# Loads of the first 256 tokens on a hardware queue, and an output product in thirds: a retention layer with a bilinear feed-forward on one core

## The chip, the core and the metric

The kernel runs on one core of a Trainium2 chip. The core has a matrix engine (PE, with its weight loads shown apart as PEld), a vector engine (DVE), a scalar engine (ACT), a general engine (POOL) and a queue engine (SP), and 16 DMA engines. Loads that POOL issues go through the software queue [...]; loads that SP issues go through the hardware queue [...]. The metric is the time on the device in microseconds; before the change it is 335.84, the median of four runs (335.33 to 339.21).

## The reference

```
scores = q @ k^T / 8                  # 8 batches, 8 heads, 576 positions, 64 per head
ret    = (scores * Dmat) @ v          # Dmat[i, j] = gamma_h ** (i - j) for i >= j, else 0
x      = ret, heads side by side      # 4608 tokens x 512
out    = ((x @ w_a) * (x @ w_b)) @ w_out     # 512 -> 1536 -> 512
```

gamma of head h is 1 - 2^(-5-h). Inputs and output are fp32. The kernel multiplies in bf16 and sums in fp32. It splits the decay: v is scaled by gamma^-j, q (or the result) by gamma^i/8, and a mask of zeros and ones keeps i >= j. So a running sum of k^T v (the *state*) carries everything from earlier positions of the batch.

## The kernel before

The 4608 tokens are 36 chunks of 128. Chunks 0 to 3 are the *fresh* ones, handled as two *units* of 256 tokens, two neighbouring tokens to a partition (e = 0, 1). The later chunks go in pairs through `kv` (state sums), `stage1` (scores, and what comes from the state), `stage2` (scores times v, then the scaling into xT). The feed-forward takes 9 blocks of 512 tokens: `ffn_ab` makes, for each of 12 slices F of the 1536 inner columns, `pa` and `pb` (4 matmuls each), copies pa on ACT and multiplies on DVE into hT; `ffn_out` then makes four products `po` of 128 tokens, 12 matmuls each against w_out.

Everything is scheduled by hand: each engine executes its instructions in the order of the program, and an instruction waits until what it reads is there and what it overwrites is free.

The start is one straight sequence (lines 161 to 171 issue the first loads, lines 606 to 652 the rest). For unit 0: 9 idle products, transposes of q, an idle product, transposes of k, two idle products, scores, state; then unit 1 the same way, with the first three F of block 0 between, in halves of 256 tokens. Before the change q of unit 0 is loaded as bf16 (line 141, POOL) and is scaled as it leaves PSUM, with `qs0`, a table of 128 x 4 x 256 made by four exps on ACT (line 206):

```
    nc.vector.tensor_tensor(q_out, tq.rearrange("p c e t -> p c t e"),
                            qs0.rearrange("p c (t e) -> p c t e", e=2),
                            op=ALU.mult)
```

POOL's queue holds, in this order: q and k of unit 0, three index tables (`ramp`, line 151), the second half of v of unit 0, a table, q, k and v of unit 1, the weights of F 0 and of F 1, 2 (line 118, four loads each), the scaling of v of unit 1 (line 479), the remaining weights in three groups, w_out in one load of 3 MB (line 124), then chunks 4 to 9, v, q, k each. The first half of v of unit 0 is SP's only load.

From F 3 of block 0 on, a list `todo` with due costs sets what goes between the matmuls. A matmul of 512 columns counts 1; when the count passes an entry's cost, at an edge (after an F in `ffn_ab`, after every fourth matmul in `ffn_out`), the entry is put into the program. Block 0's `ffn_ab` ends at 96, its `ffn_out` at 144. `pop` puts single steps of the state sums at further places. Chunks 4 and 5 enter inside the first `ffn_out`: the scaling of v on DVE and `transposes` (16 on PE, copied out by ACT and DVE, lines 277 and 278) at 110 and 112, the state product at 116, `first` and `second` (stage1, stage2) at 128 and 136.

PSUM has 8 buffers of one bank: 4 in `ps_ffn` (pa, pb, po, and before the change the transposes `tp`), 2 in `ps_x` (state products and scores), 2 in `ps_o`.

Of the kernel before, what the change touches and what calls it, by code (L numbers as in the profile page):

```python
# [18 lines left out]
def kernel(  # L19
# [117 lines left out]
    def load_fresh_qk(u):  # L137
        t = [nat.tile([128, 2, DM], BF16, tag="qk", name="fqk")
             for _ in (0, 1)]
        for w, src in ((0, q), (1, k)):  # L140
            nc.gpsimd.dma_start(  # L141
                t[w].rearrange("p a b -> p (a b)").rearrange(
                    "p (h x) -> p h x", h=H),
                src[0, :, 256 * u:256 * u + 256, :].rearrange(
                    "h (p e) d -> p h (e d)", e=2))
        fresh[u] = [x.rearrange("p a b -> p (a b)").rearrange(
            "p (h e d) -> p h e d", h=H, e=2) for x in t]
# [13 lines left out]
    load_fresh_v(0, 0, 4, nc.sync)  # L161
    load_fresh_qk(0)
# [3 lines left out]
    load_fresh_v(0, 4, 8, nc.gpsimd)  # L166
    ramp(posf[:, 4 + MID + 1:NPOS], [[128, PER - MID - 1]], 64, 1)
    load_fresh_qk(1)
# [14 lines left out]
    lgq = const.tile([128, HP], FP32)  # L183
    for p in range(HP):
        for r in (0, 1):
            nc.vector.memset(lgq[64 * r:64 * r + 64, p:p + 1],
                             math.log(gammas[2 * p + r]))
# [16 lines left out]
    qs0 = const.tile([128, HP, 256], FP32)  # L204
    for p in range(HP):
        nc.scalar.activation(qs0[:, p], idx[:, 0:256], AF.Exp,
                             bias=biasq[:, 0:1], scale=lgq[:, p:p + 1])
# [6 lines left out]
    def make_keep2():  # L214
        for e in (0, 1):
            nc.vector.tensor_copy(rowf[:, e:e + 1], posf[:, 2 * e:2 * e + 1])
            nc.vector.tensor_scalar_add(
                rowf[64:128, e:e + 1], rowf[64:128, e:e + 1], -128.0)
            nc.vector.tensor_scalar(keep2[:, e, :], idx[:, 0:128],
                                    rowf[:, e:e + 1], None, op0=ALU.is_ge)  # L220
# [42 lines left out]
    def transposes(i, by_dma):  # L263
        qk = qk_of[i]
        qkT = qkt_pool.tile([128, 2, HP, 128], BF16, tag="qkT", name="qkT")
        qkt_of[i] = qkT
        if by_dma:
            nc.sync.dma_start_transpose(
                qkT.rearrange("p w c t -> p (w c) t"),
                qk.rearrange("p w e -> p (w e)"))  # L270
            return
        tp = ps_ffn.tile([128, 2, HP, 128], BF16, tag="ab", name="tp")
        for w in (0, 1):
            for p in range(HP):
                nc.tensor.transpose(tp[:, w, p, :],
                                    qk[:, w, p * 128:(p + 1) * 128], identity)
        nc.scalar.copy(qkT[:, 0], tp[:, 0])
        nc.vector.tensor_copy(qkT[:, 1], tp[:, 1])
# [152 lines left out]

    def ffn_out(blk):
        hT = hT_of.pop(blk)
        for u in range(4):
# [25 lines left out]
            osb = o_pool.tile([128, DM], FP32, tag="osb", name="osb")  # L460
            if u % 2 == 0:
                nc.scalar.copy(osb, po)  # L462
            else:
                nc.vector.tensor_copy(osb, po)  # L464
            nc.sync.dma_start(out[tok:tok + 128, :], osb)
# [8 lines left out]
    def fresh_vscale(u, h0, h1, eng):  # L474
# [3 lines left out]
        for e in (0, 1):  # L478
            eng.tensor_tensor(  # L479
                fv[u][e].rearrange("p (h d) -> p h d", h=H)[:, h0:h1, :],  # L480
                vf2[:, u, :].rearrange("p (h e d) -> p h e d", h=H, e=2)[
                    :, h0:h1, e, :],
                vs_all[:, 2 * e + u, h0:h1].unsqueeze(2).to_broadcast(
                    [128, h1 - h0, D]), op=ALU.mult)

    def fresh_transposed(u, w, p0, p1, place):
        tp = place[0].tile([128, p1 - p0, 2, 128], BF16, tag=place[1],
                           name="ftp")
        for p in range(p0, p1):
            for e in (0, 1):  # L490
                for r in (0, 1):
                    nc.tensor.transpose(
                        tp[half(r), p - p0, e, :],
                        fresh[u][w][:, 2 * p + r, e, :], identity)
# [14 lines left out]
    def fresh_kv(u, s):  # L509
        for p in range(HP):  # L510
            for e in (0, 1):
                for r in (0, 1):
# [3 lines left out]
                        fresh[u][1][half(s), h, e, :],  # L516
# [82 lines left out]
    def settled(u, n=1, w=128):  # L599
        for _ in range(n):  # L600
# [7 lines left out]
    fresh_vscale(0, 0, 4, nc.vector)  # L608
    q_out, k_out = fresh_tiles(0)
    tq = fresh_transposed(0, 0, 0, HP, AB)  # L610
    idle_products(1)
    tk = [fresh_transposed(0, 1, 0, 2, AB), fresh_transposed(0, 1, 2, 4, X)]
    make_keep2()
    nc.vector.tensor_tensor(q_out, tq.rearrange("p c e t -> p c t e"),
                            qs0.rearrange("p c (t e) -> p c t e", e=2),
                            op=ALU.mult)
    nc.scalar.copy(k_out[:, 0:2], tk[0])
    nc.vector.tensor_copy(k_out[:, 2:4], tk[1])
    make_qs(256, 512)
    idle_products(2)  # L620
    fresh_vscale(0, 4, 8, nc.vector)
# [5 lines left out]
    tk = fresh_transposed(1, 1, 0, HP, AB)  # L627
    fresh_state1(0)
    fresh_kv(0, 1)
    nc.scalar.copy(k_out, tk)  # L630
# [6 lines left out]
    fresh_stage2(0)  # L637
    fresh_scores(1, (X, O))
# [14 lines left out]
    load_wo(0, NF)  # L653
# [26 lines left out]
    def second(g):  # L680
        flush()
        stage2(units[g])
        if 4 <= g + 2 < len(units):
            kv(units[g + 2], nc.scalar)

    load(*range(4, 10))
    todo = [(110, vscale, (4, nc.vector)), (110, vscale, (5, nc.vector)),
            (110, transposes, (4, False)), (112, transposes, (5, False)),
            (116, kv, (units[0], nc.scalar)),
            (128, first, (0,)), (136, second, (0,)),  # L690
            (136, vscale, (6, nc.gpsimd)), (136, vscale, (7, nc.gpsimd)),
            (142, transposes, (6, False)), (148, transposes, (7, False)),
            (152, kv, (units[1], nc.scalar)),
# [29 lines left out]
    run(ffn_out(0))  # L723
# [38 lines left out]
```

## Time and profile before

| | |
|---|---|
| time of the profiled execution | 336.14 us |
| its span, first to last instruction | 334.4 us |
| all runs | 336.14, 339.21, 335.54, 335.33 us |
| granted PE clock | 1.00 throughout |
| PE busy | 318.6 us, 95% of the span |
| PE busy from 0 to 10, 10 to 20, 20 to 30 us | 8.10, 8.22, 9.55 us |
| PE busy from 40 to 50, 60 to 70 us | 7.89, 8.41 us |
| first pa of F 3, all 512 tokens | 23.68 us |
| first po | 40.61 us |
| w_out load, issue to landing | 14.9 us |

The time is the span and what lies around it. A line of the waits reads: engine, what it would run, what it waited for: total, times, longest. A line of the timeline reads: start, duration, engine, line, operation, result and operands, shape and count; in brackets how long the engine stood idle before, and what released it. Some matmul records are missing, so a count may be short. A DMA line on POOL is its issue only, not the transfer.

### The profile page before, as it was taken

The numbers are of one execution on the slowest core, as the hardware profiler recorded it, in microseconds if no ns is written. First come the engines' busy times: TensorE is split into PE (matmuls) and PEld (weight loads), VectorE is DVE, ScalarE is ACT, GpSimd is POOL, SyncE is SP. The second block draws the span as 40 slices with busy tenths as digits, with TensorE's granted clock in tenths as the row PEclk, the third lists the DMA queues.
The fourth block names the chain that finished last, engine by engine and source line by source line (L and its number), as shares of the span: only waits on it lengthen the run. The fifth ranks groups of instructions, "written<-read, shape, count | busy, mean of one in ns | idle before, by whom it ended". The sixth has DMA issues, their size and how long they took to land.

```text
span 334.4 us, 8797 instructions
## 1 busy us (share of the span) xinstructions
PE 318.6 (95%) x3705; PEld 166.7 (50%) x3746; DVE 165.4 (49%) x324; ACT 112.7 (34%) x233; POOL 143.9 (43%) x176
## 2 busy tenths in 40 slices
PE   7889889989999999999999999999999999999995
PEld 3564346868544444445444544454444444444443
DVE  6754336757554555356445644454445534444321
ACT  4737524545143213332332223322323133203321
POOL 8786297878658795508350837072100000000000
PEclk9999999999999999999999999999999999999999
DMA  9999999999999999906999499939900700020002
GB/s 144 202 159 191 217 178 233 172 133 159 183 187 181 131 157 239 177 1 89 121 204 96 79 115 217 98 56 136 190 0 28 132 34 1 12 86 31 2 31 94
DMA packets 116151, 40.94 MB, mean 122 GB/s; under 512 B 102992, under 2 KB 109392, under 8 KB 116112
## 3 DMA queue, kind: packets, MB, share of 16 engines
q0 software_dynamic: 80688, 23.34, 68.3%
q1 hardware_dynamic: 35280, 16.95, 27.6%
q8 instruction: 29, 0.48, 0.6%
q10 hardware_dynamic: 144, 0.10, 0.1%
q14 instruction: 10, 0.08, 0.1%
HBM read 37.75 MB, written 9.44 MB: 141 GB/s over the span
## 4 chain that ended last, share of the span: by engine, by line
PE 83%; DMA 10%; POOL 3%; issue 2%; DVE 0%; ACT 0%; POOLq 0%; ACTq 0%
PE po L453 25%; PE pa L414 25%; PE pb L422 25%; DMA wo_sb<-in_moe_w_out_dram 4%; DMA vf<-in_v_dram 2%; DMA wa_sb<-in_moe_w_a_dram 2%; PE o L339 2%; PE o L381 2%; PE kv L294 2%; DMA qk<-in_k_dram 1%; PE sc L359 1%; POOL fqk L141 1%; PE po L442 1%; POOL fvb L479 1%; POOL wb_sb L118 1%
## 5 line engine op out<-in xcount | busy, mean ns | idle before, releaser
L427 DVE TENSOR_TENSOR hT<-ha,pb 128x512 bf16<-128x512 bf16 (+1 forms) x123 | 76.5, 622 | 100.5 <-PE pb L422 86.9
L414 PE MATMUL pa<-xT,wa_sb 128*128 128x512 bf16 (+1 forms) x477 | 113.0, 353 | 3.0 <-issue 1.8
L422 PE MATMUL pb<-xT,wb_sb 128*128 128x512 bf16 (+1 forms) x491 | 113.4, 353 | 0.1
L419 ACT CAST ha<-pa 128x512 bf16<-128x512 f32 (+1 forms) x123 | 65.7, 534 | 124.6 <-PE pa L414 123.4
L453 PE MATMUL po<-wo_sb,hT 128*128 128x512 bf16 x395 | 91.1, 379 | 4.3 <-issue 2.7
L422 PEld LDWEIGHTS <-wb_sb 128*128 128x128 bf16 x492 | 48.1, 98 | 45.3 <-issue 0.3
L414 PEld LDWEIGHTS <-wa_sb 128*128 128x128 bf16 x492 | 46.8, 98 | 47.0 <-issue 3.0
L256 POOL TENSOR_TENSOR vb<-vf,vs_all 128x512 bf16<-128x512 f32 x30 | 31.6, 1060 | 76.7 <-PE o L339 42.0
L453 PEld LDWEIGHTS <-hT 128*128 128x128 bf16 x420 | 39.0, 98 | 45.9 <-DMA wo_sb<-in_moe_w_out_dram 1.7
L462 ACT COPY osb<-po 128x512 f32<-128x512 f32 x18 | 10.6, 586 | 75.1 <-PE po L453 75.1
L102 POOL DMA_DIRECT2D qk<-in_q_dram x36 | 31.1, 867 | 7.0 <-DMA wo_sb<-in_moe_w_out_dram 6.4
L110 POOL DMA_DIRECT2D vf<-in_v_dram x36 | 31.9, 889 | 1.5 <-issue 1.0
L102 POOL DMA_DIRECT2D qk<-in_k_dram x36 | 31.1, 872 | 1.1 <-DMA vf<-in_v_dram 0.5
L367 DVE TENSOR_TENSOR sT<-sc,keep 128x512 bf16<-128x512 f32 x32 | 20.6, 684 | 12.1 <-PE sc L359 12.1
L398 DVE TENSOR_TENSOR xT<-o,qs 128x512 bf16<-128x512 f32 x32 | 20.6, 684 | 11.8 <-PE o L339 10.7
L307 DVE TENSOR_TENSOR s<-kv,s 128x256 f32<-128x256 f32 x49 | 20.5, 419 | 5.8 <-ACT sbf L317 4.5
L317 ACT CAST sbf<-s 128x256 bf16<-128x256 f32 x56 | 21.1, 406 | 3.1 <-DVE s L305 2.7
L464 DVE COPY osb<-po 128x512 f32<-128x512 f32 x17 | 11.7, 687 | 19.3 <-PE po L453 19.3
L339 PE MATMUL o<-qkT,sbf 64*64 64x64 bf16 x456 | 12.1, 195 | 0.1
L339 PEld LDWEIGHTS <-sbf 64*64 64x64 bf16 x456 | 8.2, 108 | 5.7 <-issue 5.5
L381 PEld LDWEIGHTS <-vb 64*64 64x64 bf16 x512 | 6.4, 108 | 6.6 <-issue 6.6
L381 PE MATMUL o<-sT,vb 64*64 64x64 bf16 x512 | 8.1, 195 | 0.0
(75 smaller groups left out, 128.5 us busy)
## 6 DMA issues: line engine op xcount, KB each, us to landing
out_dram<-osb SPq DMA_DIRECT2D x35, 256.0 KB, 4.6
vf<-in_v_dram POOLq DMA_DIRECT2D x29, 256.0 KB, 6.4
qk<-in_q_dram POOLq DMA_DIRECT2D x28, 128.0 KB, 6.5
qk<-in_k_dram POOLq DMA_DIRECT2D x28, 128.0 KB, 7.0
wo_sb<-in_moe_w_out_dram POOLq DMA_DIRECT2D x1, 1536.0 KB, 14.9
wa_sb<-in_moe_w_a_dram POOLq DMA_DIRECT2D x6, 192.0 KB, 6.7
wb_sb<-in_moe_w_b_dram POOLq DMA_DIRECT2D x6, 192.0 KB, 7.7
vf<-in_v_dram POOLq DMA_DIRECT2D x8, 128.0 KB, 7.4
```

The costliest lines, as they stand in the source:

```text
L102: nc.gpsimd.dma_start(t[r0:r0 + n, w, :].rearrange("p (h d) -> p h d", h=H), src[b, :, s0:s0 + n, :].rearrange("h s d -> s h d"))
L110: nc.gpsimd.dma_start(t[r0:r0 + n, :].rearrange("p (h d) -> p h d", h=H), v[b, :, s0:s0 + n, :].rearrange("h s d -> s h d"))
L256: eng.tensor_tensor(vb.rearrange("p (h d) -> p h d", h=H), vf.rearrange("p (h d) -> p h d", h=H), vs[:, i % PER, :].unsqueeze(2).to_broadc ...
L317: nc.scalar.copy(sb, new)
L339: nc.tensor.matmul(o[s][half(c), ci, j, :], st[half(r), p, :], qkt_of[i][half(r), 0, p, half(s)], start=start, stop=True, skip_group_check ...
L367: nc.vector.tensor_tensor(sT[:, r].rearrange("p n c t -> p (n c) t"), sc[r].rearrange("p n c t -> p (n c) t"), keep.unsqueeze(1).to_broadc ...
L381: nc.tensor.matmul(o[s][half(c), ci, j, :], vb[half(s), 64 * h:64 * h + 64], sT[half(s), h % 2, ci, h // 2, :], start=False, stop=True, sk ...
L414: nc.tensor.matmul(pa[:, 0:n], wa_sb[:, c, fs], xT[:, c, tok0:tok0 + n], start=(c == 0), stop=(c == NC - 1))
L419: nc.scalar.copy(ha[:, 0:n], pa[:, 0:n])
L422: nc.tensor.matmul(pb[:, 0:n], wb_sb[:, c, fs], xT[:, c, tok0:tok0 + n], start=(c == 0), stop=(c == NC - 1))
L427: nc.vector.tensor_tensor(hT[:, F, off:off + n], ha[:, 0:n], pb[:, 0:n], op=ALU.mult)
L453: nc.tensor.matmul(po, hT[:, F, u * 128:(u + 1) * 128], wo_sb[:, F, :], start=(F == 0), stop=(F == NF - 1))
```

## The change

1. q of unit 0 is loaded as fp32 by SP (`fq32`), and all of v of unit 0 behind it by SP; POOL loads k first and has neither. q is multiplied by its decay on DVE as it becomes bf16, before its transposes, with the small table `qv` (128 x 2 x 8); the transposes are then copied out unscaled, half by ACT and half by DVE. `qs0` and its constants are gone. The mask's row numbers come from POOL.
2. In the start, v of unit 0 is scaled in two instructions of 128 x 512 for four of 128 x 256, the second unit's k transposes come after the state product, in two buffers, and two of the four `make_qs` exps go to ACT after unit 0's xT.
3. w_out is loaded in thirds of 4 slices F, with chunk 4 (v, q, k) after the first and chunk 5 after the second. The output of block 0 is summed in the same thirds: 4 matmuls for each of four po, then the next third; all four po are open at once and are stored in the last third.
4. Chunks 4 and 5 are transposed in `ps_x`; those of chunk 4 come due at 90, which is after the last F (96), ahead of the output product, those of chunk 5 still at 112. v of chunk 5 and some entries for chunks 6 and 7 move by a few counts.

```diff
+    fq32 = const.tile([128, 2 * DM], FP32)
...
+    def load_fresh_qk(u, w):
+
+        t = nat.tile([128, 2, DM], BF16, tag="qk", name="fqk")
+        flat = t.rearrange("p a b -> p (a b)")
+        if u == 0 and w == 0:
+            nc.sync.dma_start(fq32.rearrange("p (h x) -> p h x", h=H),
+                              fresh_src(w, u))
+        else:
+            nc.gpsimd.dma_start(flat.rearrange("p (h x) -> p h x", h=H),
+                                fresh_src(w, u))
...
-    load_fresh_v(0, 0, 4, nc.sync)
-    load_fresh_qk(0)
+    load_fresh_qk(0, 0)
+    load_fresh_v(0, 0, 8, nc.sync)
+    load_fresh_qk(0, 1)
     ramp(idx[:, 0:512], [[1, 512]], 0, 0)
     ramp(posf[:, 0:4], [[1, 2], [256, 2]], 0, 2)
     ramp(posf[:, 4:4 + MID + 1], [[128, MID + 1]], 0, 1)
-    load_fresh_v(0, 4, 8, nc.gpsimd)
+    for c in (0, 1):
+        ramp(rowf[64 * c:64 * c + 64, 0:2], [[1, 2]], 0, 2)
+    load_fresh_qk(1, 0)
     ramp(posf[:, 4 + MID + 1:NPOS], [[128, PER - MID - 1]], 64, 1)
-    load_fresh_qk(1)
+    load_fresh_qk(1, 1)
     load_fresh_v(1, 0, 8, nc.gpsimd)
...
-    qs0 = const.tile([128, HP, 256], FP32)
-    for p in range(HP):
-        nc.scalar.activation(qs0[:, p], idx[:, 0:256], AF.Exp,
-                             bias=biasq[:, 0:1], scale=lgq[:, p:p + 1])
+    qv = const.tile([128, 2, H], FP32)
+    nc.vector.tensor_tensor(
+        qv, posf[:, 0:4:2].unsqueeze(2).to_broadcast([128, 2, H]),
+        lgv.unsqueeze(1).to_broadcast([128, 2, H]), op=ALU.mult)
+    nc.scalar.activation(qv, qv, AF.Exp, bias=biasq[:, 0:1], scale=-1.0)
...
+    def ffn_out_parts(blk, parts):
+
+        hT = hT_of.pop(blk)
+        po = [ps_ffn.tile([128, 512], FP32, tag="ab", name="po")
+              for _ in range(4)]
+        for f0, f1 in parts:
+            for u in range(4):
+                for F in range(f0, f1):
+                    nc.tensor.matmul(po[u], hT[:, F, u * 128:(u + 1) * 128],
+                                     wo_sb[:, F, :],
+                                     start=(F == 0), stop=(F == NF - 1))
+                    if F < f1 - 1:
+                        yield 1.0, False
+                if f1 == NF:
+                    store(512 * blk + 128 * u, po[u], u)
+                pop()
+                yield 1.0, True
...
-    fresh_vscale(0, 0, 4, nc.vector)
+    make_keep2()
+    for h0 in (0, 4):
+        nc.vector.tensor_tensor(
+            fresh[0, 0][:, h0:h0 + 4],
+            fq32.rearrange("p (h e d) -> p h e d", h=H, e=2)[:, h0:h0 + 4],
+            qv.rearrange("p e h -> p h e")[:, h0:h0 + 4].unsqueeze(3)
+            .to_broadcast([128, 4, 2, D]), op=ALU.mult)
     q_out, k_out = fresh_tiles(0)
-    tq = fresh_transposed(0, 0, 0, HP, AB)
+    tq = [fresh_transposed(0, 0, 0, 2, AB), fresh_transposed(0, 0, 2, 4, X)]
     idle_products(1)
+    nc.scalar.copy(q_out[:, 0:2], tq[0].rearrange("p c e t -> p c t e"))
+    nc.vector.tensor_copy(q_out[:, 2:4], tq[1].rearrange("p c e t -> p c t e"))
     tk = [fresh_transposed(0, 1, 0, 2, AB), fresh_transposed(0, 1, 2, 4, X)]
-    make_keep2()
-    nc.vector.tensor_tensor(q_out, tq.rearrange("p c e t -> p c t e"),
-                            qs0.rearrange("p c (t e) -> p c t e", e=2),
-                            op=ALU.mult)
     nc.scalar.copy(k_out[:, 0:2], tk[0])
+    fresh_vscale(0, 0, 8, nc.vector, (0,))
     nc.vector.tensor_copy(k_out[:, 2:4], tk[1])
-    make_qs(256, 512)
+    fresh_vscale(0, 0, 8, nc.vector, (1,))
+    make_qs(256, 512, (0, 1))
     idle_products(2)
-    fresh_vscale(0, 4, 8, nc.vector)
...
-    tk = fresh_transposed(1, 1, 0, HP, AB)
     fresh_state1(0)
     fresh_kv(0, 1)
-    nc.scalar.copy(k_out, tk)
+    tk = [fresh_transposed(1, 1, 0, 2, AB), fresh_transposed(1, 1, 2, 4, X)]
+    nc.scalar.copy(k_out[:, 0:2], tk[0])
+    nc.vector.tensor_copy(k_out[:, 2:4], tk[1])
...
     fresh_stage2(0)
+    make_qs(256, 512, (2, 3))
...
-    load_wo(0, NF)
...
-    load(*range(4, 10))
-    todo = [(110, vscale, (4, nc.vector)), (110, vscale, (5, nc.vector)),
-            (110, transposes, (4, False)), (112, transposes, (5, False)),
+    PARTS = ((0, 4), (4, 8), (8, NF))
+    load_wo(*PARTS[0])
+    load(4)
+    load_wo(*PARTS[1])
+    load(5)
+    load_wo(*PARTS[2])
+    load(*range(6, 10))
+    todo = [(90, vscale, (4, nc.vector)),
+            (90, transposes, (4, False, ps_x, "x")),
+            (108, vscale, (5, nc.vector)),
+            (112, transposes, (5, False, ps_x, "x")),
             (116, kv, (units[0], nc.scalar)),
             (128, first, (0,)), (136, second, (0,)),
...
-    run(ffn_out(0))
+    run(ffn_out_parts(0, PARTS))
```

## The prediction

> **What bounds the kernel now.** I read the page first, for the share of the engines.
>
> ```profile
> span 334.4 us, 8797 instructions
> ...
> PE 318.6 (95%) x3705; PEld 166.7 (50%) x3746; DVE 165.4 (49%) x324; ACT 112.7 (34%) x233; POOL 143.9 (43%) x176
> ```
>
> PE is busy for 318.6 of 334.4 us, so at most 15.8 us can be won without taking matmuls away, and the change takes none away: the two builds have 7494 PE instructions each. The question is where PE stands still. The waits of PE between 24 and 100 us answer for the body:
>
> ```profile
> PE pa L414 <- issue: 1.6, 1, 1.6
> PE tp L275 <- DMA qk<-in_k_dram: 1.5, 1, 1.5
> PE po L453 <- DMA wo_sb<-in_moe_w_out_dram: 1.2, 1, 1.2
> ```
>
> Each is one wait (total, times, longest). Two are loads. The third is a gap that no releaser explains. The timeline shows the two loads in place, and POOL's queue beside them:
>
> ```profile
> 33.57 0.91 POOL L110 DMA_DIRECT2D vf<-in_v_dram  x1 [1.01 <-issue]
> ...
> 40.61 3.63 PE L453 MATMUL po<-wo_sb,hT 128*128 128x512 bf16 x16 [1.23 <-DMA wo_sb<-in_moe_w_out_dram]
> 40.86 0.88 POOL L102 DMA_DIRECT2D qk<-in_q_dram  x1 [6.38 <-DMA wo_sb<-in_moe_w_out_dram]
> ...
> 41.73 0.88 POOL L102 DMA_DIRECT2D qk<-in_k_dram  x1
> ...
> 46.36 0.40 PE L275 MATMUL tp<-identity,qk 128*128 128x128 bf16 x4 [1.45 <-DMA qk<-in_k_dram]
> ```
>
> PE waits for the whole w_out, and POOL, which has issued v of chunk 5, may not issue its q and k until w_out has landed. So k of chunk 5 starts at 41.73 and PE waits for it at 46.36. Counting POOL's issues, every wait of this kind fits one rule: a load waits for the one eight before it (w_out is the 27th, q of chunk 5 the 35th; the 14th waits for the 6th, v of unit 1).
>
> The start is a chain too. From the chain of waits, in order of time:
>
> ```profile
> 5.00 1.68 POOL fqk L141 x2
> 6.68 6.64 DMA vf<-in_v_dram
> 13.32 0.28 issue
> 13.60 0.62 POOL wb_sb L118
> 14.22 0.01 issue
> 14.23 2.06 POOL fvb L479 x2
> ```
>
> v of unit 1 lands at 13.3, POOL scales it until 16.29, PE starts unit 1's state product at 16.5, and only then may the next weights be issued. The DMA column of one-microsecond windows shows lost time before that chain (last two numbers: DMA share, GB/s):
>
> ```profile
> 2.00:3.00 1.00, 1.00 (x4) 0.43 (x3) 0.67 (x10) 0.02 (x1) 1.00 (x2) 1.00 0.82 242
> 3.00:4.00 1.00, 1.00 (x4) 0.33 (x3) 0.00 (x0) 0.00 (x0) 0.94 (x4) 1.00 0.55 51
> ```
>
> The hardware queue moves its 256 KB between 2 and 3 us, and then the engines nearly idle until the software queue's q arrives.
>
> [...] the write rate rises from 207 to 310 GB/s at 38 to 39 us, as v of chunk 4 starts on some engines, while w_out completes only at 40.56; so a load can trail by about 1.5 us. [...] line 256 on DVE shows 691 to 693. [...] Here DVE's copy of a tp (58.07) starts only as ACT's (57.45 for 0.59) ends.
>
> **The start, part by part.** SP issues q and v of unit 0 from 0.74 (0.46 each). POOL loses two issues (1.06 and 0.81) and gains two iotas of about 0.1, so k of unit 0 is issued at 1.27 for 2.32, q of unit 1 near 3.5 for 4.90, and v of unit 1 near 5.4 for 6.68. Bytes read until v of unit 1 lands stay six times 512 KB. What changes is that the engines have work at 3 to 4 us: 51 for 242 GB/s is 0.8 us of moving. I take 0.8 for the landing of v of unit 1, and so for all loads after it on POOL; bounds 0 (packets only swapped) and 1.4 (POOL's head start).
>
> On PE: q lands 1.1 us later than the half v did (256 KB more at 242 GB/s; 0.74+2.7+1.1, 4.5 us). DVE decays it in two instructions of 0.69 (about 4.6 to 6.0), each releasing eight transposes (half of 1.06); ACT and DVE copy the halves (0.59; 0.42 as L618, up to 0.69 since the write is strided). qT is ready near 7.2, for 7.10+1.23, 8.33. But k lands no earlier than about 7, then come its 16 transposes, and DVE's queue now has a v scale of 0.69 ahead of its half of k: near 8.6. Two idle products stand before the scores, which start near 9.0 for 9.42, and their masks (4 of 0.62) end near 11.9 for 12.58. So unit 0 gains 0.4 to 0.7, and unit 1 is held by v: 16.29 becomes 15.5. I take 0.8 for the start.
>
> Costs at nothing: four exps (2.06) leave ACT and one of 128x16 comes, all while it waits for PE; eight memsets (0.74) and four small row operations (0.15 each) leave DVE, before q has landed. Two exps of make_qs (0.52 each) move to after unit 0's xT on ACT, ahead of the first ha; they end near 15.0, when its pa does, and if that cover is gone cost 0.2 at most. The weights of F 3 landed at 24.4 with PE asking at 24.5: no margin, so PE's 0.8 counts only because these loads move by the same 0.8.
>
> **w_out in thirds.** Its rate: the last earlier weight lands near 33.0, w_out at 40.56: 3146 KB in 7.6 us, 415 GB/s. A third takes 2.5 us. A chunk is 786 KB; q and k of chunk 4 with v of chunk 5 took from about 41.6 to 43.5, so about 2.5 with its start. With everything 0.8 earlier: first third 34.7, chunk 4 37.2, second third 39.7, chunk 5 42.2, last third 44.7, each up to 1.5 later by its slowest engine. Eight loads back never holds these: v of chunk 5 waits for the first third, the last third for q of chunk 4.
>
> PE ends the first products at 39.38-0.8, 38.6, and now has chunk 4's transposes there (0.45), then 16 matmuls (3.45), chunk 5's transposes (0.45), 16, 16. Chunk 4 has 1.4 spare; the second third is needed at 42.9 (3.2 spare); chunk 5 at 42.5 (0.3 spare: I charge 0.4, bounds 0 and 1.2); the last third at 48 (3 spare). Both waits go: 1.23+1.45. What queues behind a late chunk 4 on PE is the whole output product.
>
> **Other places.** The transposes write ps_x for ps_ffn, since four po hold all of ps_ffn. kv needs both ps_x buffers, four matmuls (0.86) after the transposes; their copies take 0.06+0.59+0.02+0.42, 1.1. PE waits 0.3 (0.2 to 0.5). In before, the output copy of 48.99 stood ahead of the state sums on DVE, and PE waited 0.26 at 50.96 for the last; stores now come in the last third, so that goes. Four stores at the end, 0.86 apart, on ACT (0.59) and DVE (0.69): the next pa and pb take the po buffers in that order, 0.43 apart, behind the copies; nothing, or 0.3 if a copy is late. SP has the four stores ahead of the first transposing DMAs in both kernels.
>
> **Sum.** 0.8+1.23+1.45+0.26-0.4-0.3 = 3.04. Against the profiled execution's 336.14 (334.4 span, 1.74 around): 333.10. That execution stands 0.30 above the median, 335.84; so 332.8. The unexplained 1.58 at 67.62 I leave; it may go, or come twice.
>
> **Rivals.** *All lands early* (0.24): the start gives 1.4, chunk 5 is in time, and perhaps the 1.58 goes: 3.04+0.6+0.4 is 331.8, with the gap 330.2. For it: the gap has no releaser. Against: it sits where no edit is. *Chunk waits take over* (0.17): engines don't keep the order, chunk 4 lands only with the second third, 39.7 plus 1: PE waits 2.1 ahead of the products, 334.9. For it: the 1.5 of trailing. Against: the q and k of chunk 4, right behind w_out, were there at 43.86. *Slower* (0.06), by chunk 4 too: its transposes were 16 matmuls into the product, now ahead of it, and each microsecond late costs one. k of chunk 4 later than 38.6+3.04, 41.6, makes it slower; in before it took up to 3.3 after w_out, here 34.7+1.5+3.3, 39.5. At 43, 337.2. That the start does nothing leaves 333.6, inside the forecast.
>
> **Chances.** Forecast 0.53, from 331.9 to 334.2. A measurement here tells about 1% from no change, 332.5 on the fast side. A third of the forecast lies below it, and the first rival: 0.41. Slower by over 1% takes half of the last: 0.03. The rest 0.56. The range 330.8 to 335.2 leaves out the lower part of the first rival, the tail of the second and the last: some 0.2.
>
> **What would show it.** Right: no wait of po for wo_sb, none over 0.5 at the two tp; v of unit 1 at about 12.5 and F 3 at about 22.9. Wrong: a tp that waits over 1 us for in_k; F 3's pb waiting for wb_sb; k of unit 0 after 8 us.

## The result and the profile after

The changed kernel has a median of 340.11 us (334.96 to 343.84, 43 executions) where the kernel before has 336.25 us (334.14 to 343.6, 64 executions). The two profiled executions are 337.12 us (span 335.3) and 336.14 us (span 334.4). The ratios given here leave out executions that lie far above the fastest of their kernel (22 of the 44 listed of the changed kernel, 9 of the 123 of the kernel before that ran beside the experiments), and so stand nearer to 1 than the medians do. The ratio is 1.0035, with a 95% interval of 1.0015 to 1.0055: a third of a per cent slower. The medians of all executions are 3.86 us apart, 1.1%, so the change may cost more than the ratio says. The forecast was 332.8 with a range of 330.8 to 335.2; it was wrong, and in direction too.

The page of the kernel after, first its engines and then the granted PE clock in 40 slices of 8.4 us:

```profile
span 335.3 us, 8789 instructions
...
PE 320.2 (95%) x3705; PEld 168.3 (50%) x3746; DVE 165.3 (49%) x314; ACT 111.1 (33%) x231; POOL 143.7 (43%) x178
...
PEclk9859999999999999999999999999999999999999
```

PE is busy for 1.6 us more with the same matmuls, and two of the first three slices are below full clock; before, all forty were at 9.

**The thirds did what they were for.** The waits of PE between 24 and 100 us, for the kernel after:

```profile
PE pa L417 <- issue: 2.3, 1, 2.3
PE po L482 <- issue: 0.5, 3, 0.2
PE po L451 <- issue: 0.2, 1, 0.2
```

The wait of po for w_out and that of tp for k of chunk 5 are gone. The timeline of the kernel after, at the head of the output product:

```profile
42.55 0.61 PE L278 MATMUL tp<-identity,qk 128*128 128x128 bf16 x8
42.99 3.62 PE L451 MATMUL po<-wo_sb,hT 128*128 128x512 bf16 x16
46.45 0.61 PE L278 MATMUL tp<-identity,qk 128*128 128x128 bf16 x8
46.89 1.03 PE L451 MATMUL po<-wo_sb,hT 128*128 128x512 bf16 x3
47.85 0.66 PE L297 MATMUL kv<-vb,qk 64*64 64x64 bf16 x24
```

No line carries a bracket: nothing waits. But the first po starts at 42.99, where it started at 40.61 before, although no wait for w_out precedes it any more. PE came late.

**The start lost what the thirds won.** The timeline of PE in the kernel after, at four places:

```profile
8.02 1.06 PE L516 MATMUL ftp<-identity,fqk 128*64 128x128 bf16 x16 [0.79 <-DMA fqk<-in_k_dram]
...
16.81 0.39 PE L417 MATMUL pa<-xT,wa_sb 128*128 128x256 bf16 x2 [1.09 <-issue]
...
27.00 1.03 PE L417 MATMUL pa<-xT,wa_sb 128*128 128x512 bf16 x3
...
70.12 0.28 PE L417 MATMUL pa<-xT,wa_sb 128*128 128x256 bf16 x1 [2.27 <-issue]
```

The same four places before are 7.46, 15.75, 23.68 and 69.20. The second and the last are the two gaps that nothing in the profile explains; they stand at the same instruction in both kernels. They cut the difference into parts:

| stretch | before | after | difference |
|---|---|---|---|
| up to the end of the first gap | 15.75 | 16.81 | +1.06 |
| from there to the first pa of F 3 | 7.93 | 10.19 | +2.26 |
| from there to the start of the last gap | 43.94 | 40.85 | -3.09 |
| the last gap | 1.58 | 2.27 | +0.69 |
| sum | | | +0.92 |

The span grew by 0.9. Ahead of F 3 PE lost 3.32 where I had forecast a gain of 0.8; from there to the last gap it won 3.09, in part only because it came late (the halves below tell how much). Of the 1.06 only 0.23 is there when PE reaches its first pa (15.32 for 15.09 us); the other 0.83 is the longer gap behind it (1.09 for 0.26). One-microsecond windows of the kernel after (second column PE's busy time; the last three numbers are clock, DMA share and GB/s) show the 2.26:

```profile
7.00:8.00 1.00, 0.23 (x1) 0.00 (x0) 1.00 (x2) 0.00 (x0) 1.00 (x2) 0.78 1.82 180
8.00:9.00 1.00, 0.98 (x16) 0.82 (x16) 0.24 (x1) 0.30 (x1) 1.00 (x3) 0.50 1.81 180
...
20.00:21.00 1.00, 1.00 (x6) 0.71 (x5) 0.00 (x0) 0.37 (x1) 1.00 (x2) 0.50 1.14 169
```

The clock is 0.50 from about 7.6 to 11 and again from about 17.8 to 24.6. In those windows four pa of 256 columns take 1.04 us, where they take 0.60 at full clock. Half clock for these 10.2 us is 5.1 us of full clock lost (not all on the path), or 0.015 of the span, as the mean clock of 0.985 of this execution has it. It is no accident of one execution: the mean clock is below 0.986 in 30 of the 44 executions of this kernel that are listed, and in 16 of 123 of the kernel before that ran beside the experiments.

Last, the loads of the start. The windows from 2 to 4 us of the kernel after, and POOL's wait for v of unit 1:

```profile
2.00:3.00 1.00, 1.00 (x4) 0.43 (x3) 0.20 (x2) 0.02 (x1) 0.92 (x3) 1.00 0.45 117
3.00:4.00 1.00, 1.00 (x4) 0.33 (x3) 0.88 (x5) 0.43 (x2) 0.94 (x5) 1.00 1.13 342
```

```profile
5.37 0.90 POOL L131 DMA_DIRECT2D vf<-in_v_dram  x1
...
13.38 0.61 POOL L118 DMA_DIRECT2D wb_sb<-in_moe_w_b_dram  x1 [1.52 <-DMA vf<-in_v_dram]
```

The hole at 3 to 4 us is filled (342 for 51 GB/s), as I expected, though the microsecond before it moves less (117 for 242). v of unit 1 is issued 1.3 us earlier (5.37 for 6.68). It is there at 13.38 for 13.60. Of 1.3 us of lead, 0.2 arrived in this pair. Over the four profiles of each start in which nothing shifts it, POOL's wait ends at 13.60 to 14.10 with the old start (before, `cool`, `thirds_again`, `thirds_only`) and at 13.19 to 13.38 with the new one (after, `start_only`, `warm_early`, `fill_late`): about 0.6 earlier in the middle. That PE had no use for it is shown in the step-by-step account.

### The profile page after: what moved, and what is told of

Read it like the earlier page. It is cut to its first block, busy times and chain, and to the rows that moved or that the text cites. A ratio compares the mean times of both kernels' runs of the same rounds, so it can differ in the third digit from the quotient of the medians.

```text
span 335.3 us, 8789 instructions
## 1 busy us (share of the span) xinstructions
PE 320.2 (95%) x3705; PEld 168.3 (50%) x3746; DVE 165.3 (49%) x314; ACT 111.1 (33%) x231; POOL 143.7 (43%) x178
## 4 chain that ended last, share of the span: by engine, by line
PE 94%; issue 2%; DMA 2%; ACT 1%; ACTq 0%; POOLq 0%
PE pa L417 28%; PE pb L425 28%; PE po L482 24%; PE po L451 3%; DMA fqk<-in_k_dram 2%; PE o L342 2%; PE o L384 2%; PE kv L297 2%; PE sc L362 1%; PE po L471 1%; PE tp L278 1%; PE ftp L516 0%; PE fo L596 0%; PE fsc L573 0%; PE kv_sum L538 0%
## 5 line engine op out<-in xcount | busy, mean ns | idle before, releaser
L482 PEld LDWEIGHTS <-hT 128*128 128x128 bf16 x372 | 34.7, 98 | 39.6
L370 DVE TENSOR_TENSOR sT<-sc,keep 128x512 bf16<-128x512 f32 x32 | 20.6, 684 | 13.4 <-PE sc L362 13.3
```

The source lines that it names most:

```text
L370: nc.vector.tensor_tensor(sT[:, r].rearrange("p n c t -> p (n c) t"), sc[r].rearrange("p n c t -> p (n c) t"), keep.unsqueeze(1).to_broadc ...
L482: nc.tensor.matmul(po, hT[:, F, u * 128:(u + 1) * 128], wo_sb[:, F, :], start=(F == 0), stop=(F == NF - 1))
```

## The experiments

Three theories went into them. *C*, the clock: the new start leaves PE idle between 4.8 and 8 us, the clock falls to half, and that eats the gain. *L*, the loads: k of unit 0 and v of unit 1 come no earlier, and that is the whole cost. *F*, instructions: the gaps without a releaser are PE waiting for a block of its own instructions, which stand at fixed places of its program and come through the same DMA engines as the data. The idle products that some kernels add or drop have no use in the result.

### The two halves apart

`thirds_only` is the kernel before with points 3 and 4 of the change; `start_only` is the changed kernel with w_out in one load and the old output product.

```diff
 thirds_only, on the kernel before
-    load_wo(0, NF)
...
-    load(*range(4, 10))
+    PARTS = ((0, 4), (4, 8), (8, NF))
+    load_wo(*PARTS[0])
+    load(4)
+    load_wo(*PARTS[1])
+    load(5)
+    load_wo(*PARTS[2])
+    load(*range(6, 10))
...
-    run(ffn_out(0))
+    run(ffn_out_parts(0, PARTS))
```

> The kernel before with the second half of the change alone (w_out in thirds, chunks 4 and 5 between, transposes in ps_x). Theory C (the new start leaves PE idle, its clock falls to half, and that eats the gain): this half keeps its gain of about 2.9 us, so 0.991 of before, no wait of po for wo_sb, clock 1.00. Rival L (the gain of the thirds is only what a late PE finds already loaded): with PE 3 us earlier than in the whole change the waits come back at the transposes, 0.996 to 1.000.

> The changed kernel with w_out in one load and the output product as before: the first half of the change alone. Theory C: the first pa of F 3 at about 27 us for 23.7, clock about 0.985, but w_out has landed by the time PE comes and the wait of 1.2 goes: 1.003 to 1.010 of before. Rival L (k of unit 0 and v of unit 1 landing no earlier are the whole cost, under 1 us): 0.998 to 1.002.

`thirds_only`: median 335.37 (333.66 to 342.21, 6 executions), ratio 0.998 (0.9925 to 1.0035); profiled 334.44, span 332.7. `start_only`: median 337.81 (335.85 to 344.17, 20 executions), ratio 1.0023 (0.9996 to 1.0051). The halves point in opposite directions, but both intervals hold 1, and 0.991 had been expected of `thirds_only`. The waits of PE between 24 and 100 us, first `thirds_only`, then `start_only`:

```profile
PE pa L414 <- issue: 1.6, 1, 1.6
PE tp L275 <- DMA qk<-in_k_dram: 0.5, 1, 0.5
```

```profile
PE pa L417 <- issue: 2.7, 1, 2.7
PE tp L278 <- DMA qk<-in_k_dram: 2.2, 1, 2.2
PE po L482 <- DMA wo_sb<-in_moe_w_out_dram: 1.1, 1, 1.1
PE tp L278 <- DMA qk<-in_q_dram: 0.3, 1, 0.3
PE kv L297 <- issue: 0.2, 1, 0.2
```

The thirds alone take both load waits away but for 0.5 us. The new start alone keeps both. Two places of each, first `thirds_only`, then `start_only`:

```profile
23.96 1.03 PE L414 MATMUL pa<-xT,wa_sb 128*128 128x512 bf16 x4
...
67.41 0.28 PE L414 MATMUL pa<-xT,wa_sb 128*128 128x256 bf16 x1 [1.58 <-issue]
```

```profile
16.29 0.39 PE L417 MATMUL pa<-xT,wa_sb 128*128 128x256 bf16 x2 [0.44 <-issue]
...
24.23 1.03 PE L417 MATMUL pa<-xT,wa_sb 128*128 128x512 bf16 x4
```

In `thirds_only` the stretch from the first pa of F 3 to the start of the last gap takes 41.87 us, in `thirds_again` below 41.72, for 43.94 before and 40.85 in the changed kernel. So the thirds give 2.07 and 2.22 by themselves; the rest of the 3.09, about 0.9 to 1.0 us, is waiting that a late PE no longer has to do.

`start_only` has the start of the changed kernel. Its clock falls once, from 8.6 to 12 us, and is then 1.00 until 49 us. From the end of the first gap to F 3 it takes 7.94 us, as the kernel before does (7.93), where the changed kernel took 10.19. So the 2.26 of the table above is the second fall of the clock, and where that fall stays away the new start brings PE to F 3 only 0.55 us later (24.23 for 23.68). Theory C had expected that pa at about 27 and no wait for w_out; in this execution neither came.

Because its interval held 1, `thirds_only` ran again:

> The thirds of w_out on the start of before, a second time, for its interval. If the thirds are the gain and the new start the loss: the runs at full clock 333.5 to 334.5, the ratio of the runs 0.993 to 0.998 with its interval below 1.000, and the share of runs with a mean clock below 0.986 near that of before (12 of 75). If PE's lead is taken back by loads anyway: ratio 0.998 to 1.002. If the clock falls by chance whatever the start: half the runs below 0.986, as in the first six.

Ratio 0.9965 (0.9935 to 0.9994), 22 executions. The four with a mean clock over 0.9965 took 333.0 to 334.5 (median 333.7), and four of 22 fell below 0.986. So by this ratio the thirds alone are a third of a per cent faster than the kernel before, and their mean clock is below 0.986 more often than that of before (with the first six, 7 of 28 for 16 of 123) and far less often than that of the changed kernel (30 of 44). Yet the median of all 22, 337.57, is above that of the 48 executions of before beside it, 336.62: over all executions a gain is not shown. What takes it back is seen below, under the loads of k.

### The clock

```diff
 warm_early, on the changed kernel
-    idle_products(9)
+    idle_products(12)
...
-    idle_products(1)
+    idle_products(4)

 fill_late, on warm_early, inside the scores of a unit
         for e in (0, 1):
+            if (u, e) == (1, 1):
+                late_products(12)

 cool, on the kernel before
-    idle_products(9)
+    idle_products(7)
...
-    idle_products(1)
```

> The changed kernel with three more idle products ahead of q's transposes (12 for 9) and three more ahead of k's (4 for 1), which fill the idle stretches of PE at 4.8 to 5.9 and 7.2 to 8.0 us. Theory C: no half clock between 7.6 and 10.8, and with the scores 0.5 earlier perhaps none at 17.9 either: 332.5 to 335 us, 0.990 to 0.996 of before. If the second fall has its own cause (the idle stretch at 15.7 to 16.8), it stays and the gain is under 1.5 us. Rival L: the clock doesn't matter, the same as the changed kernel or up to 0.5 us slower.

> The kernel before with less idle work: 7 idle products for 9, and none between the transposes of q and k. Only work whose result nobody uses is gone. Theory C: PE stands idle for about 1.6 us before q lands, the clock falls to half in the start of some or all executions, and the kernel is slower by 1 to 5 us (1.003 to 1.015). Rival L: the same time as before within 0.2%.

> The changed kernel with the six early idle products of the run before and 12 idle products of 256 columns (0.11 us each) ahead of the second half of unit 1's scores, where PE otherwise waits for xT (0.45) and then for an unexplained gap of 1.8. Theory F (PE's instructions come in blocks, one block boundary lies in unit 1's scores or first pa, and the next block isn't there before about 16 us): PE is held there until about 15.9 with or without the products, so they cost nothing. With theory C (clock): the window before is now busy, so the clock doesn't fall at 15.5; first pa of F 3 at about 24.3 for 27.6, and 334 to 336.5 us for 338.8 to 342.9. Rival (the gap is work that PE hasn't shown, not a fixed point in the instructions): 1.3 us later, and no better than the run before.

`warm_early` was to mend the start and made it worse: median 341.07, ratio 1.0141 (1.0087 to 1.0195). Its first fall of the clock is gone and unit 0's scores start at 9.01 for 9.98, but now PE waits 1.84 us without a releaser in unit 1's scores, and the clock falls there. `fill_late` differs from it only by 12 idle products of 256 columns ahead of the second half of those scores: median 339.55, ratio 1.001 (0.9978 to 1.0042); it loses again farther on, where k is late (below). Five-microsecond windows, with the granted clock third from the end, first `warm_early`, then `fill_late`:

```profile
15.00:20.00 5.00, 3.60 (x53) 2.51 (x53) 1.71 (x3) 0.74 (x2) 5.00 (x9) 0.51 0.89 119
20.00:25.00 5.00, 5.00 (x59) 3.55 (x59) 1.71 (x3) 1.12 (x3) 3.64 (x7) 0.50 1.27 187
```

```profile
15.00:20.00 5.00, 3.32 (x77) 2.56 (x79) 1.61 (x3) 1.49 (x4) 5.00 (x9) 1.00 0.92 125
20.00:25.00 5.00, 4.60 (x75) 3.86 (x75) 2.90 (x7) 1.49 (x4) 3.46 (x7) 1.00 1.24 181
```

The clock is 1.00 instead of 0.50, and the first pa of F 3 comes at 24.71 for 27.64. The gap itself ends no earlier (16.21 for 15.93). So the clock alone is worth 2.9 us in this stretch; theory C holds for it. The executions agree: the mean clock is below 0.986 in all four of `warm_early` and in 4 of 20 of `fill_late`. The two together also tell which fall is dear. `warm_early` fills the waits for q and k and has no fall at 7.6 us, and the fall behind the gap still comes; `fill_late` fills the place of the gap, and that fall goes.

`cool` was to bring the fall into the kernel before by taking three idle products away, and did not: median 336.16, ratio 0.9989 (0.9961 to 1.0017), the profiled clock 1.00. PE is busy there for 2.05 of the 4 us from 4 to 8; in the changed kernel it is 1.90 and the clock fell, but in the profile of `thirds_only` it is 2.09 and the clock fell as well (0.50 from 8 to 10). And in one kernel below PE stood still for 2.23 us on end at full clock. So idle PE brings the fall about in these runs, since filling prevents it (1.00 for 0.50 above), but the busy time of any one stretch of 4 us doesn't tell when.

No long wait stands ahead of the falls at 7.6 and 17.8 us: in the changed kernel the longest single waits there are 1.14 and 1.09 us. In `thirds_again` below the clock fell 2.5 us into one wait.

The traces show more of when it falls. Ten of the profiles have sixteen falls between them, all in the first 100 us. Worked out from the clock column, each lasts 3.4, 6.8 or 10.2 us, and those of one execution start whole steps of 3.41 us apart: at 7.55 and 17.79 in the changed kernel (three steps), at 8.59, 49.55 and 73.44 in `start_only` (twelve and seven). Where the steps lie differs from one execution to the next. With windows of that length laid on these steps, PE was busy for 0.07 to 0.58 of the window ahead of every fall (0.52 and 0.55 in the changed kernel). Of the windows at full clock that no fall follows, only two are in that range (0.51 and 0.54, at 66 us in `warm_early` and `thirds_only`); all others are at 0.59 or more. So in these runs a fall took no window that was idle throughout; about four tenths of one was enough. That a given wait does it or not by where the steps lie is my inference from this, and no run tests it.

### The gaps without a releaser

`warm_early` adds six products, 12 instructions with their weight loads; both gaps then stand 12 instructions earlier in PE's program. `cool` removes three, and the later gap stands 6 instructions later. So they keep to a count of instructions, not to a piece of work. The page of before has a line for a queue that I had passed over (packets, MB, share of 16 engines):

```profile
q8 instruction: 29, 0.48, 0.6%
```

0.48 MB in 29 packets are some 16.5 KB each. PE with its weight loads has 7451 instructions on the same page, and no other engine more than 324; if the packets are PE's, that is an estimate of 257 instructions to a packet. The two shifted kernels below, with some 150 more for PE, have 30 packets. The transfers in windows of 0.2 us show when each starts; for the kernel before, 13.2 to 13.4 us, and for the kernel after, 14.2 to 14.4:

```profile
q0 software_dynamic: 131, 0.04, 173.4%
q8 instruction: 1, 0.02, 29.8%
```

```profile
q0 software_dynamic: 77, 0.04, 137.1%
q8 instruction: 1, 0.02, 27.9%
```

Each packet stands among those of the software queue. Here is every gap over 0.2 us at pa, pb, scores or state products up to 75 us, with the packet ahead of it:

| kernel | packet starts | gap ends | between | gap |
|---|---|---|---|---|
| before | 13.2; 66.8 | 15.75; 69.20 | 2.5; 2.4 | 0.26; 1.58 |
| after | 14.2; 67.8 | 16.81; 70.12 | 2.6; 2.3 | 1.09; 2.27 |
| start_only | 13.8; 70.4 | 16.29; 73.31 | 2.5; 2.9 | 0.44; 2.68 |
| thirds_only, thirds_again | 65.0; 63.8 | 67.41; 66.30 | 2.4; 2.5 | 1.58; 0.73 |
| warm_early | 13.6; 69.4 | 15.93; 72.41 | 2.3; 3.0 | 1.84; 4.38 |
| cool | 65.2 | 68.08 | 2.9 | 1.28 |
| fill_late | 13.8; 62.4 | 16.21; 65.28 | 2.4; 2.9 | 1.58; 0.28 |
| late_w1 | 12.6; 69.6 | 15.12; 72.66 | 2.5; 3.1 | 0.96; 3.65 |
| thirds_v | 65.6 | 68.43 | 2.8 | 2.05 |

The gap ends 2.3 to 3.1 us after the packet starts, in all of them, however long it is. The record doesn't name the engine that a packet is for; that it is PE's is inferred from this, from the number of packets and from the moved counts. In these sixteen places the packet started less than 2.3 to 3.1 us before PE's arrival, and PE waited. The changed kernel's first packet starts 1.0 us later than that of before, and so does its second.

Two more kernels move the places and one relieves the engines:

```diff
 shift_rows, on the changed kernel (thirds_shift: the first line on thirds_only); a narrow product
 is 64 x 64 x 64, and 80 of them are 160 instructions with their weight loads, for 18
-    idle_products(9)
+    narrow_products(80)
...
-    idle_products(1)
+    idle_products(4)

 late_w1, on warm_early
-    load_w(128, 384)
...
     fresh_vscale(1, 0, 8, nc.gpsimd)
+    load_w(128, 384)
```

> The changed kernel with 80 narrow idle products (64 x 64) in place of the first nine wide ones and 4 for 1 in the middle: PE's instruction stream is 148 longer ahead of the rest, so a block boundary no longer lies in unit 1's scores or first pa, nor the later one at the same place. Theory F: no unexplained gap of PE over 0.5 between 10 and 20 us; both gaps move by 148 instructions or go. With the clock kept: 332.5 to 335 us. If the narrow products don't count as work for the clock: warm only later, 335 to 338. Rival: a gap of about 1 us stays in unit 1's scores or the first pa.

> The thirds alone on the kernel before, with the 80 narrow idle products in place of the first nine: 142 instructions longer ahead of the rest. Theory F: the gap of 1.6 near 67 us goes or shrinks below 0.8, and none at 15: 331.5 to 334, 0.987 to 0.994 of before. Rival: the gap of 1.6 stays at the same matmul, 333.5 to 335.

> The changed kernel with the six early idle products and the weights of F 1 and 2 issued after the scaling of v of unit 1, so the DMA engines are nearly empty from about 13.5 to 16. Theory F with the loads as its cause (the block waits behind the queued loads): the gap in unit 1's scores falls from 1.8 to under 0.7, and PE is then held by the weights of F 1 instead, so the whole is slower. Rival (the block comes a fixed time after it is asked for, whatever the loads do): the gap stays at 1.5 to 2.

Both shifted kernels have no gap of this kind left, at 16 or at 70 us: theory F holds. `late_w1` (one execution, 341.75) leaves the DMA engines empty from 14 to 16 us. Its packet starts 1.0 earlier than in `warm_early`, 12.6 for 13.6, and the gap is 0.96 for 1.84; but from the packet's start PE still takes 2.5 us. It loses elsewhere, since pa and pb wait 0.7 and 1.6 us for the delayed weights, and its clock falls too. So in this pair the loads delay the packet's start, and not what follows it. Whether the 1.0 us between the kernels before and after has the same reason is not shown.

And yet the shifted kernels gained nothing: `shift_rows` 339.69 (ratio 1.0111, 1.0043 to 1.0179), `thirds_shift` 338.96 (1.0035, 1.0004 to 1.0065). Part of it lies in the start: in `thirds_shift` k of unit 1 holds PE for 2.23 us (at full clock throughout), and its first pa of F 3 is at 24.68 for 23.96. The rest is the next section.

### What takes the place of the later gap

The timeline of `thirds_shift`, the state products of the pairs that follow:

```profile
80.89 0.31 PE L294 MATMUL kv<-vb,qk 64*64 64x64 bf16 x8 [0.81 <-DMA qk<-in_k_dram]
...
91.56 0.32 PE L294 MATMUL kv<-vb,qk 64*64 64x64 bf16 x16 [2.90 <-DMA qk<-in_k_dram]
```

Without the gap PE reaches the pair before these at 70.37, where `thirds_only` does at 72.43, 2.06 earlier; then it waits 3.71 us for k. The spans are 334.6 and 332.7. In all profiles of the study long waits for k stand where the gap is short or missing:

| kernel | gap without a releaser, 60 to 75 us | waits of kv for k, 70 to 97 us |
|---|---|---|
| warm_early, late_w1, start_only, after, thirds_v | 4.38, 3.65, 2.68, 2.27, 2.05 | none |
| before, thirds_only | 1.58, 1.58 | none |
| cool | 1.28 | 1.2 |
| thirds_again, fill_late | 0.73, 0.28 | 4.2, 4.4 |
| thirds_shift, shift_rows, shift_fill | none | 3.7, 5.5, 7.1 |

POOL issues the loads of a pair only behind the scaling of v of an earlier pair, ahead of which it stands still each time (2.16 and 2.44 us before the scalings at 78.66 and 88.52 of `thirds_shift`), and k takes some 7 us from issue to landing (median 7.2 from 50 to 80 us in the changed kernel). So from 60 to 95 us PE runs close behind its loads. A lead of PE is one half of it; the other is when the loads ran. In `thirds_only` the scaling of v that the loads of these pairs stand behind starts at 65.42 us, in all the others between 66.81 and 70.39 (67.60 in `thirds_shift`). So the kernels that came early mostly found their k late, and `thirds_only` kept its lead in an execution whose loads were early.

A wait of that length also cost clock here. `thirds_again` and `thirds_only` are the same program, run on two chips; PE is at the same place at 89.4 us in both profiled executions, but POOL's scalings of v ahead of the loads start at 69.57, 80.39 and 90.31 us in the second, for 65.42, 76.27 and 85.80. The first of these followed a wait of 5.13 us for v to land; why v came later that time is open. First `thirds_only`, then `thirds_again`:

```profile
89.41 0.50 PE L294 MATMUL kv<-vb,qk 64*64 64x64 bf16 x32
89.84 3.63 PE L479 MATMUL po<-wo_sb,hT 128*128 128x512 bf16 x16
```

```profile
89.37 0.32 PE L294 MATMUL kv<-vb,qk 64*64 64x64 bf16 x16
93.69 0.43 PE L294 MATMUL kv<-vb,qk 64*64 64x64 bf16 x16 [4.00 <-DMA qk<-in_k_dram]
```

Windows of `thirds_again`, with the clock third from the end:

```profile
90.00:92.00 2.00, 0.00 (x0) 0.00 (x0) 0.89 (x2) 0.00 (x0) 1.69 (x2) 1.00 2.26 182
92.00:94.00 2.00, 0.31 (x16) 0.30 (x16) 0.00 (x0) 0.00 (x0) 2.00 (x4) 0.55 1.25 122
94.00:96.00 2.00, 2.00 (x17) 0.74 (x6) 0.85 (x2) 0.01 (x1) 2.00 (x3) 0.50 1.75 182
```

The last products start at 333.14 for 326.47: 6.67 us, of which 4.00 are the wait and the other 2.67 the half clock from 92 to 99 us, as no other wait follows in either. So two executions of one program can differ by this much through one late k. Behind the later gap the clock can fall too: it is 0.50 for 3.4 us between 69 and 77 us in `start_only`, `warm_early`, `thirds_v` and `late_w1`, with gaps of 2.05 to 4.38; behind the 2.27 of the changed kernel's profiled execution it stayed at 1.00.

### Both causes of the start at once, and v alone

```diff
 shift_fill, on shift_rows: the late_products(12) of fill_late

 thirds_v, on thirds_only
-    load_fresh_v(0, 0, 4, nc.sync)
+    load_fresh_v(0, 0, 8, nc.sync)
...
-    load_fresh_v(0, 4, 8, nc.gpsimd)
```

> The changed kernel with both causes taken away that the traces show in its start: narrow idle products move the place where PE waits for an instruction packet, and twelve idle products of 256 columns stand before the second half of unit 1's scores. If packet and clock are the start's loss: no gap without a releaser at 14 to 18 us, clock 1.00 until 26 us, first pa of F 3 at 23.7 to 24.4 (25.69 with the narrow products alone, 24.71 with the filling alone). If the loads of unit 0 and 1 are the loss: 25 or later with the clock at 1.00. For the whole kernel: if the lead is kept, 333.5 to 335; if the loads of k are the next bound, kv waits for in_k for 3 us or more between 73 and 95 us, and the time is 336.5 to 338.5.

> The thirds on the start of before, and of the new start only that the second half of v of unit 0 comes on the hardware queue too; q stays on the software queue. If my 0.8 us was right for v and spoilt by q as fp32: v of unit 1 ready on POOL 0.5 to 0.8 earlier than with the thirds alone, and the first pa of F 3 at 22.3 to 22.8 (23.10 there), 333.0 in the runs at full clock. If the bytes ahead of v of unit 1 set its landing whatever the queue: within 0.2 of the thirds alone, 333.7.

`shift_fill` (median 339.89, ratio 1.0058, 1.0016 to 1.01) has no gap in the start and the clock at 1.00 until 26 us. Its first pa of F 3 comes at 24.66, between my two expectations. Of its four waits between 10 and 30 us, two are for loads or what stands behind them:

```profile
PE ftp L516 <- DMA fqk<-in_k_dram: 1.1, 1, 1.1
PE kv_sum L538 <- POOL fvb L503: 0.8, 1, 0.8
```

Those are k and v of unit 1: POOL waits for v until 14.79 in this execution. With clock and packet mended, the new start is still 1.0 us behind the old one, and theory L holds for what it waits for here. But in all three shifted kernels v is later than without the shift (14.29 to 14.81 for 13.19 to 14.10), so part of this may come with the shift; `fill_late`, not shifted, is as far behind (24.71) with v there at 13.21. Farther on kv waits 7.1 us for k, and takes the rest.

`thirds_v` puts only the second half of v of unit 0 on the hardware queue: median 337.9, ratio 1.0026 (1.0000 to 1.0053). v of unit 1 is issued at 5.86 for 6.66 in `thirds_again`, and POOL's wait for it ends at 14.19 for 13.97. Issued 0.8 earlier, landed no earlier. What the engines moved more from 2 to 5 us (206 for 142 GB/s) they moved less from 5 to 8 (171 for 224). The v that now comes in one piece is there only at 4.97, DVE starts its scaling there for 4.50, and unit 0's transposes start at 6.87 for 6.01. The longer wait ends in a clock of 0.50 from 8 to 14 us, and the first pa of F 3 comes at 25.52 for 23.85 (the 23.10 of my expectation is no time of that pa in either profile of the thirds).

## Why the prediction was wrong, step by step

**The start, 0.8 (bounds 0 and 1.4): wrong in sign.** This is the step that failed: it let PE gain what v of unit 1 gains ("unit 1 is held by v: 16.29 becomes 15.5"). The timeline of the kernel before doesn't have that wait:

```profile
15.98 0.60 PE L422 MATMUL pb<-xT,wb_sb 128*128 128x256 bf16 x4
16.51 0.44 PE L514 MATMUL kv_sum<-fvb,fqk 64*64 64x64 bf16 x16
```

POOL is ready at 16.29, and PE comes to the state product at 16.51, straight from its pb, without a bracket; the margin is small (in `thirds_only`, with v there at 14.10, PE waited 0.21), but it is no wait to be won. All its waits from 9.4 us to F 3 are for ACT, DVE or the gap. So an earlier v could bring w_out and the weights forward, but not PE; and PE's own way to F 3 became longer, by 0.23 at the first pa, 0.83 in the gap and 2.26 in the clock.

The loads themselves came nearer to the forecast. The hole at 3 to 4 us was filled, and v came 0.22 earlier in the profiled pair and about 0.6 over four profiles of each start, for my 0.8. The working counted the bytes read (six times 512 KB in both); q as fp32 also writes 512 KB where bf16 wrote 256 (the sizes that the pages list for its load, from SP after and from POOL before), and up to 13 us the changed kernel moves 0.30 MB more than the kernel before (2.57 for 2.27 MB, the sum of the one-microsecond windows from 2 us). That fits, but `thirds_v` writes nothing more and has no earlier v at all, so the width of q is not the whole reason; what fixes the landing stays open. My figure for q was low as well (DVE starts on it at 5.14, not 4.5), and k of unit 0 came at 8.0, which I had named as a sign of being wrong.

**What the step left out was larger than what it had.** I bounded the cost of a late start by its waits. The waits of 1.14 and 0.79 us for q and k stand ahead of the first fall of the clock, which cost little: `start_only` has it too and is at its first pa at 15.46, 0.37 later than before. The dear fall is the second, behind the gap of 1.09: 2.26 us up to F 3 in the profiled execution, and `fill_late` against `warm_early` gives 2.9 for such a fall. I had read "granted clock 1.00 throughout" as a fact about the kernel, when it was one about an execution: 16 of 123 others of the same kernel have a mean clock below 0.986.

**The gap of 1.58 us, "I leave".** It could be read: the page listed the queue, and the gap is the packet's start plus 2.3 to 3.1 less PE's arrival. In the changed kernel it costs 0.69 more, and the small one at 15.75, which I didn't name, 1.09 for 0.26. The rival *all lands early* had priced it as 1.58 to be won; in `thirds_shift` taking it away was worth nothing, since k was late in its place.

**The thirds: right, in mechanism and in size.** The sum gave 1.23+1.45+0.26-0.4-0.3, 2.24. With the start of before they measured 2.07 and 2.22. There chunk 5 was late by 0.54 and 0.62, near the 0.4 charged for it, while kv didn't wait for ps_x (0.3 charged). The 3.09 of the changed kernel is more because PE came late: chunk 5 was then in time (no wait at 46.45). Without both charges the sum is 2.94, and 0.15 is not accounted for. The prediction's own case "that the start does nothing leaves 333.6" is what the thirds alone take at full clock: 333.7, in four executions of 22.

**The rivals.** *Chunk waits take over* and *slower, by chunk 4* both put the risk into the output product, where nothing went wrong. The measured outcome, a start that loses more than the thirds win, had no case of its own; the start was held to be worth at least 0.

## What to carry to other kernels

Before an earlier load is counted as time, look whether the matrix engine waits for it at that place: v of unit 1 came earlier, and in the kernel before PE did not stand still for it. A start that left the matrix engine waiting a little more could cost its clock for 3.4 to 10 us in these runs, and behind the gap of 1.09 us that was 2.26 us, more than the wait itself: keep it fed through the start, and price a wait with the clock that may follow. A gap without a releaser that stays at one count of instructions was here, as far as the runs tell, a block of instructions on its way (sixteen gaps ended 2.3 to 3.1 us after its packet started); look for its packet before you take the gap for free time, and ask what stands behind it, because here k was late in its place (3.7 to 7.1 us of waiting in the shifted kernels). Moving a load to another queue brought its landing forward by less than its issue: an issue 0.8 us earlier landed no earlier, and one 1.3 us earlier landed 0.2 earlier in the profiled pair, about 0.6 over four profiles of each start.

## What the runs showed that I had not expected

- The queue `q8 instruction` moved 29 packets of some 16.5 KB among the data, most likely PE's instructions. From the packet's start to PE's next instruction passed 2.3 to 3.1 us in sixteen gaps, also where the DMA engines were empty for the latter half of it (`late_w1`, 2.5). With the weights of F 1 and 2 queued (`warm_early`) the packet started 1.0 us later than without.
- The falls of the PE clock lasted 3.4, 6.8 or 10.2 us and started whole steps of 3.41 us apart, which lay differently in each execution. All sixteen came behind a step in which PE was busy for 0.58 or less; only two such steps had no fall behind them. Standing still for 2.23 us on end in `thirds_shift` brought none; in `thirds_again` the clock fell 2.5 us into a wait of 4.00.
- Two executions of one program differed by 6.6 us through a single late k: 4.0 of waiting, 2.7 of clock.
